# Batches 4 to 7: eight heads' scores in one run on 64 rows of the array, both groups' reads in another, attention recorded visits ahead

## The chip, the cores and the metric

The kernel runs on one core of a Trainium2 chip. The metric is the device time of one execution in microseconds. Three runs of the kernel before gave a median of 700.7 us (698.89 to 702.76).

## The reference, cut to what matters

There are two stages. An attention between 512 tokens and 32 states per head gives, per batch, 544 rows; a gated layer without an activation function runs over all 8 x 544 = 4352 of them.

```
B, H, S, Ns, D = 8, 8, 512, 32, 64            # x: [B, H, S, D], state: [B, H, Ns, D]
scores  = scale * x @ state.T                  # softmax over the states
xread   = softmax(scores) @ state
scores2 = scale * state @ x.T                  # the same scores, turned; softmax over the tokens
sread   = softmax(scores2) @ x
attn = concat([xread, sread], axis=2)          # [B, H, S + Ns, D]
x = attn.transpose(0, 2, 1, 3).reshape(B * (S + Ns), H * D)
out = ((x @ w_a) * (x @ w_b)) @ w_out          # 512 -> 1536 -> 512
```

## The kernel before, in words

**The tokens.** xread is never made. Since xread @ w_a is softmax(scores) @ (state @ w_a), the kernel makes the products P = state @ [w_a, w_b] per head (`project`), writes them to a scratch tensor `scr` in DRAM, and for each batch and chunk c of the 1536 columns reads them back (`p_raw`). `layer1` multiplies them with the weights of the softmax, which stand transposed in `at_h` and `at_l` ([4 heads x 32 states, group, 512 tokens]). Numbers are kept as a high and a low fp32r part, so each product is three matmuls: high x high, high x low, low x high. `layer2` multiplies the gated result (`g_h`, `g_l`) with `w_out` (tiles `wo`), sums over the chunks in four accumulators `acc`, and parks partial sums (`stg`, `part`) between visits.

**The states.** sread is made outright. The reads of all batches gather in the tile `xst`, and `States` runs the gated layer over these 256 rows.

**Attention, per batch and group of four heads** (`Attention`). A batch has two groups, g = 0 and 1. `load` brings x transposed with the states beside it (`x_raw`, 128 rows = two heads x 64). `scores` makes the four heads' scores with four fp32 matmuls into 32 partitions each of one PSUM tile `ms`: all 128 rows of the array are used, and the states of the head that isn't meant are zeros. `soft` takes the maximum over the tokens, and ScalarE the exponential with its sum (tile `e2`, one buffer). In parallel `turn`, `exp`, `norm` and `back` make the token side's softmax and write `at_h` and `at_l`. `reads` transposes the exponentials with four matmuls and copies them to `a2`; `nat` loads x untransposed; `sread` makes the reads with 16 small matmuls (4 token blocks x 4 heads); `scaled` divides by the sum and writes the result twice beside itself; `keep` transposes it with one matmul (`ms<-ident,a`), and two copies of VectorE put it into `xst`.

**The order.** `VISITS` lists which batch does which chunks, and where the states' visits (SU) stand. Batch 4 is first visited in visit 9, batch 5 in 15, batch 6 in 17, batch 7 in 19; the first states' visit is 16. `attend(b)` records a batch's attention just ahead of its first visit, and that of batches 6 and 7 ahead of visit 16, since `tokens` needs all reads. From batch 3 on (`JOINED`) `end_reads(a.scores)` records the reads of the group before and the scores of the next group as one unit, so that TensorE changes only once between its two kinds of matmul.

All work is recorded first, as units with a cost and a due time, and `plan` then orders it: backwards it gives each unit its latest start (`late`), and forwards it picks on each engine the ready unit with the earliest one. The table `SHIFTS` adds a number to the `late` of some runs of units, in hundreds of nanoseconds. `paced` gives the layers' matmuls due times from a clock. Buffers of a name go round in the order of recording; tiles of `stg` (four buffers) and `ms` (two) are free of that order. DMAs are all issued by SP.

Of the kernel before, what the change touches and what calls it, by code (L numbers as in the profile page):

```python
# [20 lines left out]
P = 128  # L21
TOK = S + NS
NG = 2
# [22 lines left out]
WIDE = (0, 1)  # L46

JOINED = 3

# [108 lines left out]
class Unit:  # L158


    def __init__(self, eng):
        self.eng, self.calls, self.acc, self.touch = eng, [], [], []
        self.occ = self.lat = 0.0
        self.base = None
        self.turned = False


class Recorder:
# [31 lines left out]
    def cost(self, u, eng, method, out, ins, kw):  # L200
        n = 1
        sh = (out if isinstance(out, View) else ins[0]).where()[0]
        for x in sh[1:]:
            n *= x
        ps = bool(ins) and ins[0].tile.pool.name.startswith("ps")
        if eng == "PE":
            if method == "transpose" or kw.get("is_transpose"):
                o = n * .85
            elif ins[-1].dtype == F32R:
                o = (n + 32) / 2.4  # L210
            else:
                o = n / .6
            if sh[0] < P:
                o *= sh[0] / P
            if method == "matmul" and "is_transpose" not in kw and ins[-1].dtype == F32 and not u.turned:
                o, u.turned = o + 370, True
            lat = o + 172
        elif eng == "ACT":
            if method == "activation":
                o, lat = (870, 960) if "accum_out" in kw else (560, 660)  # L220
            elif ps:
                o, lat = 466 * n / 512 + (60 if n < 300 else 0), 587 * n / 512 + (80 if n < 300 else 0)
            else:
                o, lat = 522 * n / 512, 100 + n * 1.015
            if n < 8:
                o, lat = 60, 80
        elif eng == "DVE":
            if method.startswith("tensor_scalar") and not ps:
                o, lat = (65, 140) if n <= 1 else (75, 166) if n <= 16 else (333 * n / 512, 419 * n / 512)
            elif method == "tensor_reduce":  # L230
                o, lat = 593, 676
            elif method == "transpose":
                o, lat = 628, 704
            elif method == "reciprocal":
                o, lat = (72, 154) if n == 1 else (162, 244)
            else:
                o, lat = 65 + n * 1.045, 155 + n * 1.045
        elif eng == "SP":
            o = 440
            v = out if isinstance(out, View) else ins[0]  # L240
            u.bytes = 4
            for x in v.where()[0]:
                u.bytes *= x
            u.load = isinstance(out, View) and out.tile.pool.name != "dram"
            u.serve, u.land = u.bytes / 428 + (0 if u.load or u.bytes < 4e5 else 240), 1560 if u.load else 900
            lat = 980 + u.serve + u.land
        else:
            o, lat = 1000, 1060
        if eng in ("ACT", "DVE") and out.tile.name.startswith("sd_") and len(out.where()[0]) == 4:
            o, lat = 2 * o, 2 * lat  # L250
        if eng in ("ACT", "DVE"):
            o, lat = o * SLACK, lat * SLACK
        if u.calls[:-1]:
            u.lat = u.occ + lat
            u.occ += o
        else:
            u.occ, u.lat = o, lat
# [8 lines left out]
class Engine:  # L266
# [13 lines left out]


SHIFTS = {
# [12 lines left out]
}  # L295


# [9 lines left out]
def plan(units, pools, t0):  # L307
# [23 lines left out]
    for p in pools:  # L331
        for tag, tiles in p.tags.items():
            tiles = [t for t in tiles if t.uses]
            for j, t in enumerate(tiles):
                first = min(t.uses)
                opens.setdefault(first, []).append(t)
                for k in set(t.uses):
                    edge(first, k, False)
                if t.free:
                    continue  # L340
                if j:
                    edge(min(tiles[j - 1].uses), first, False)
                if j >= t.bufs and tag not in LOOSE:
                    for k in set(tiles[j - t.bufs].uses):
                        edge(k, first)

    left = [len(x) for x in suc]
    order = [i for i in range(n) if not left[i]]
# [113 lines left out]
def attn_moe(ctx, tc, xt, xn, sd, wl, w_out, out):  # L462
# [26 lines left out]
    def f32(ap):  # L489
        return ap.bitcast(F32)  # L490
# [89 lines left out]

    scr = [[dram.tile([NG, 4, 4, NS, 512], F32, name=f"scr{c}_{g}") for g in range(2)] for c in range(NC)]
    w = {}

# [25 lines left out]
    def project(c, hp, bg, hh, psp, tag):  # L611
        if hh == 0:
            name, bufs = SW[st["n"] % len(SW)]
            st[bg], st["n"] = proj.tile([P, 2, 512], F32, name=name, bufs=bufs), st["n"] + 1
        sw = st[bg]
        ps = psp.tile([P, 512], F32, name=tag)
        with rec.together(sw):
            for cols, r in columns(c, hp, hh):
                for k, s in enumerate((sd_h, sd_l)):
                    nc.tensor.matmul(ps[:, cols], lhsT=s[hp // 2][:, 2 * (hp % 2) + hh, bg], rhs=r,  # L620
                                     start=(k == 0), stop=(k == 1))
        nc.scalar.copy(out=sw[:, hh], in_=ps)
        if hh:
            h = 2 * (hp % 2)
            nxt.extend(lambda i=i: nc.sync.dma_start(
                out=scr[c][bg][hp // 2, :, h + i].rearrange("b n x -> n b x"), in_=sw[:, i]) for i in range(2))


    xst = const.tile([P, 4, B, NS], F32, name="xst")
# [10 lines left out]
    def load_a(b):  # L640
        new_a(b)
        for i in range(2):
            nc.sync.dma_start(out=f32(a_t[b][i]), in_=a_dram[b][i])

    class Attention:

# [15 lines left out]
        def scores(self):  # L662
# [5 lines left out]
            with rec.together(self.e2, *(() if self.b in WIDE else (self.sp,))):  # L668
                for hq in range(4):
                    n = slice(hq * NS, (hq + 1) * NS)  # L670
                    nc.tensor.matmul(self.s[n], lhsT=self.st[:, hq // 2, hq % 2 * NS:(hq % 2 + 1) * NS],
                                     rhs=self.x[:, hq // 2], start=True, stop=True)

        def scores_t(self, psp, tag):

# [62 lines left out]

        def reads(self):
            ps = ps_ms.tile([P, 512], F32, name="ms")  # L740
            self.a2 = att.tile([P, 4, P], F32, name="a2", bufs=1)
            with rec.together(self.a2):
                for sb in range(4):
                    nc.tensor.transpose(ps[:, sb * P:(sb + 1) * P], self.e2[:, sb * P:(sb + 1) * P], ident)
# [20 lines left out]
        def scaled(self):  # L765
            ps, m2 = self.s, self.m2
            nc.vector.tensor_scalar_add(out=m2[:, 3:4], in0=m2[:, 2:3], scalar1=EPS)
            nc.vector.reciprocal(out=m2[:, 3:4], in_=m2[:, 3:4])

            nc.scalar.mul(out=self.a2[:, 0, :].rearrange("p (t d) -> p t d", t=2),  # L770
                          in_=ps[:, :D].unsqueeze(1).broadcast_to([P, 2, D]), mul=m2[:, 3:4])

        def keep(self):
            ps = self.s
            nc.tensor.transpose(ps[:, P:2 * P], self.a2[:, 0, :], ident)
            for hh in range(2):
                rows = slice(hh * D, (hh + 1) * D)
                nc.vector.tensor_copy(
# [137 lines left out]

    clock = [0.0]

    def paced(f, *args):
        u = f(*args[:1], **args[1])  # L920
        u.base = clock[0]
        clock[0] += u.occ * PACE

# [70 lines left out]
    def end_reads(*more):  # L994
# [7 lines left out]
            a.keep()  # L1002
        pending.clear()

    def attend(b):
        if b not in a_t:
            new_a(b)
        for g in range(NG):
            a = atts[b, g]
            a.load()  # L1010
# [73 lines left out]
    for v, (u, cs) in enumerate(VISITS):  # L1084
# [11 lines left out]
        elif not earlier:  # L1096
# [3 lines left out]
                    ready.add(b)  # L1100
            end_reads()
            unit.tokens()
        clock[0] = max(clock[0], STARTS.get(v, 0.0))
        for i, c in enumerate(cs):
            if u != SU:
# [66 lines left out]
```

## Time and profile before

| | before |
|---|---|
| median of three runs | 700.7 us |
| the profiled execution: time | 700.03 us |
| its span, first to last instruction | 698.2 us |
| mean granted clock of TensorE | 0.999 |
| bytes read from and written to HBM | 87.03 and 46.66 MB |

The profile is one execution; its times count from the start of the span. PE is TensorE's matmuls, PEld its weight loads, DVE is VectorE, ACT is ScalarE, SPq SP's queue of DMA issues. A row of the timeline has the start, the time to the end of the last of its instructions, the engine, the line, the operation, the output and input tiles, the shapes and the count. All instructions are issued on one line, 1129, so rows are told apart by tiles. An fp32 matmul leaves two records in the trace, so that 16 matmuls read as x32. A row of the windows has the stretch, then for each engine the busy time and the number of instructions, then the granted clock, the DMA engines' share and GB/s.

### The profile page before, as it was taken

Reading aid. Unit: us, or ns where it says so; the run is one execution under the profiler, and the core shown is the slowest. Engines: PE = TensorE matmul, PEld = TensorE weight load, DVE = VectorE, ACT = ScalarE, POOL = GpSimd, SP = SyncE. Lnnn points to the kernel's source line nnn. Section 1 sums busy time; section 2 is a strip of 40 time slices with the busy share of each in tenths; the row PEclk is TensorE's granted clock in tenths of the full one; section 3 lists DMA queues with packets and bytes.
Section 4 is the critical chain, followed back from the end, with each engine's and each line's share of the span. In section 5 each row is a group of like instructions: output and inputs, shape, how many; then the busy total and the mean of one; then the engine's idle time right before and its main releaser. Section 6 shows DMA issues by size and latency. Waiting matters only on the chain.

```text
span 698.2 us, 10183 instructions
## 1 busy us (share of the span) xinstructions
PE 677.7 (97%) x3712; PEld 543.2 (78%) x3712; DVE 486.5 (70%) x947; ACT 394.3 (56%) x727; POOL 0.7 (0%) x6
## 2 busy tenths in 40 slices
PE   4899999999999999999999999999999999999997
PEld 1576767887878888788888877877798888988886
DVE  5999788889986775745997367558869734884321
ACT  6988967898764667754543344334555433552322
POOL 0000000000000000000000000000000000000000
PEclk9999999999999999999999999999999999999999
DMA  8689977899495757768995144234244312500002
GB/s 325 243 295 336 338 248 243 307 319 393 163 335 204 271 171 251 252 232 263 392 332 158 59 155 125 95 120 139 82 152 150 109 43 61 181 31 30 1 0 92
DMA packets 55090, 134.36 MB, mean 192 GB/s; under 512 B 5632, under 2 KB 5632, under 8 KB 55040
## 3 DMA queue, kind: packets, MB, share of 16 engines
q1 hardware_dynamic: 55040, 133.71, 55.1%
q8 instruction: 29, 0.48, 0.3%
q14 instruction: 21, 0.17, 0.1%
HBM read 87.03 MB, written 46.66 MB: 191 GB/s over the span
## 4 chain that ended last, share of the span: by engine, by line
PE 88%; ACT 5%; DMA 5%; issue 1%; SPq 1%; DVE 0%; DVEq 0%
PE ab L1129 41%; PE acc L1129 38%; PE ms L1129 9%; ACT wq L1129 2%; DMA p_raw<-scr 1%; DMA p_raw<-sd 1%; DMA scr<-sw_st 1%; DMA part<-stg 1%; DMA scr<-wo 1%; SPq L1129 1%; ACT t L1129 1%; ACT sd_h L1129 0%; ACT wo L1129 0%; ACT sw_st L1129 0%; ACT g_h L1129 0%
## 5 line engine op out<-in xcount | busy, mean ns | idle before, releaser
L1129 PE MATMUL acc<-wo,g_h 128*128 128x512 f32 x816 | 249.0, 392 | 0.0
L1129 PEld LDWEIGHTS acc<-wo,g_h 128*128 128x128 f32 x816 | 151.6, 188 | 31.7 <-issue 0.8
L1129 DVE TENSOR_TENSOR a_sb<-ab,a_sb 128x512 f32<-128x512 f32 (+1 forms) x108 | 71.2, 659 | 130.2 <-PE ab L1129 115.2
L1129 PE MATMUL ab<-at_h,p_h 128*128 128x512 f32 x384 | 149.7, 394 | 2.4 <-ACT p_h L1129 2.4
L1129 PE MATMUL acc<-wo,g_l 128*128 128x512 f32 x408 | 150.9, 392 | 0.0
L1129 PE MATMUL ab<-at_l,p_h 128*128 128x512 f32 x384 | 149.6, 393 | 0.0
L1129 PE MATMUL ab<-at_h,p_l 128*128 128x512 f32 x384 | 148.8, 392 | 0.0
L1129 ACT COPY a_sb<-ab 128x512 f32<-128x512 f32 (+1 forms) x108 | 61.0, 565 | 137.6 <-PE ab L1129 137.0
L1129 ACT CAST g_h<-a_sb 128x512 fp32r<-128x512 f32 (+1 forms) x108 | 64.7, 599 | 59.5 <-DVE a_sb L1129 50.1
L1129 PEld LDWEIGHTS acc<-wo,g_l 128*128 128x128 f32 x408 | 76.6, 188 | 19.1 <-issue 2.5
L1129 DVE TENSOR_TENSOR g_l<-a_sb,g_h 128x512 fp32r<-128x512 f32 (+1 forms) x108 | 70.7, 655 | 28.1 <-ACT g_h L1129 21.3
L1129 PEld LDWEIGHTS ab<-at_h,p_h 128*128 128x128 f32 x384 | 72.2, 189 | 23.2 <-ACT p_h L1129 3.5
L1129 PEld LDWEIGHTS ab<-at_h,p_l 128*128 128x128 f32 x384 | 72.3, 189 | 16.0 <-issue 0.8
L1129 PEld LDWEIGHTS ab<-at_l,p_h 128*128 128x128 f32 x384 | 72.2, 189 | 15.3 <-issue 0.8
L1129 ACT CAST p_h<-p_raw 128x512 fp32r<-128x512 f32 x92 | 53.4, 621 | 24.5 <-PE ab L1129 16.0
L1129 DVE TENSOR_TENSOR p_l<-p_raw,p_h 128x512 fp32r<-128x512 f32 x92 | 60.1, 682 | 6.0 <-ACT p_h L1129 5.8
L1129 DVE TENSOR_SCALAR t<-t 128x512 int32<-128x512 int32 x120 | 49.6, 420 | 13.4 <-ACT t L1129 10.8
L1129 ACT CAST wq<-t 64x512 fp32r<-64x512 f32 (+1 forms) x64 | 38.7, 619 | 4.4 <-PE ab L1129 1.7
L1129 DVE SCALAR_TENSOR_TENSOR t<-raw,t 128x512 int32<-128x512 int32 (+1 forms) x60 | 39.5, 684 | 0.2
L1129 PE MATMUL ms<-wq,sd_h 128*128 128x512 f32 (+2 forms) x112 | 38.0, 412 | 0.3 <-ACT a L1129 0.2
L1129 PE MATMUL ms<-wq,sd_l 128*128 128x512 f32 (+2 forms) x112 | 37.4, 403 | 0.0
L1129 DVE TENSOR_TENSOR stg<-acc,stg 128x512 f32<-128x512 f32 x44 | 28.4, 683 | 9.2 <-PE acc L1129 9.2
(97 smaller groups left out, 671.4 us busy)
## 6 DMA issues: line engine op xcount, KB each, us to landing
p_raw<-scr SPq DMA_DIRECT2D x46, 512.0 KB, 4.0
scr<-sw_st SPq DMA_DIRECT2D x48, 256.0 KB, 5.1
scr<-wo SPq DMA_DIRECT2D x48, 256.0 KB, 4.2
raw<-wl SPq DMA_DIRECT2D x22, 512.0 KB, 6.1
part<-stg SPq DMA_DIRECT2D x20, 512.0 KB, 5.6
stg<-part SPq DMA_DIRECT2D x20, 512.0 KB, 5.0
out<-stg SPq DMA_DIRECT2D x34, 256.0 KB, 2.1
x_raw<-xt SPq DMA_DIRECT2D x14, 576.0 KB, 4.0
```

Source lines behind the costliest of these rows:

```text
L1129: getattr(obj, method)(*map(real, args), **{k: real(x) for k, x in kw.items()})
```

## The change

For batches 4 to 7 (`WHOLE = B // 2`) a class `Inputs` and a function `attend_whole` take the place of the steps above.

- **Groups are made anew**: a group is now heads 0, 2, 4, 6 or 1, 3, 5, 7 of the batch, that is, the upper or the lower 64 rows of the loads. The stores to `scr` follow.
- **Scores**: both halves of x are loaded (`x_raw`, and a tile of `stg` with the states in a buffer of `e2`). Eight matmuls of 64 rows follow in one unit: those of rows 0 to 63 into one tile `ms`, those of 64 to 127 into another.
- **Reads**: both groups' x is loaded (`x_nat` and a tile of `stg`), the second group's transposed exponentials go to the buffer of `x_raw`, and all 32 read matmuls are one unit into one tile, 64 columns per group.
- **Scaling and keeping**: each group scales 64 columns, once; one transpose and one copy put both groups into `xst`.
- **When**: `AHEAD` records batch 4 at visit 7, batch 5 at 14 and batch 6 at 15; batch 7 stays ahead of 16. A field `after` keeps a batch's scores behind the last layer matmul that was due by then, and all its units are due 6 us later. The cost of a matmul on 64 rows is halved.
- `SHIFTS` has new numbers for all the program.

```diff
+WHOLE = B // 2
+AHEAD = {7: 4, 14: 5, 15: 6}
...
+            if method == "matmul" and isinstance(kw.get("lhsT"), View) and kw["lhsT"].where()[0][0] < P:
+                o /= 2
...
 SHIFTS = {
-    2: -1852, 7: 155, 8: 101, 12: 125, 13: -1927, 18: -166, 24: 194, 25: 125, 27: 16, 28: -291, 35: 29, 36: 59,
...
+    1: -900, 2: -777, 7: 466, 8: -739, 11: 204, 13: -900, 23: -898, 27: 900, 32: -163, 34: -785, 36: -864, 37:
...
+    for i, u in enumerate(units):
+        if u.after is not None:
+            edge(place[id(u.after)], i, False)
...
-                out=scr[c][bg][hp // 2, :, h + i].rearrange("b n x -> n b x"), in_=sw[:, i]) for i in range(2))
+                out=(scr[c][bg][i, :, hp] if bg else scr[c][bg][hp // 2, :, h + i]).rearrange("b n x -> n b x"),
+                in_=sw[:, i]) for i in range(2))
...
+    class Inputs:
...
+        def load(self):
+            x = att.tile([P, 2, S + D], F32, name="x_raw", bufs=1)
+            nc.sync.dma_start(out=x, in_=xt[self.b, 0])
+            x1 = mlp.tile([P, 2, DM], F32, name="stg", bufs=4)
+            st = att.tile([P, S], F32, name="e2", bufs=1)[:, :2 * D].rearrange("p (a d) -> p a d", a=2)
+            by_halves(nc.sync.dma_start(out=x1, in_=xt[self.b, 1, :, :, :S]))
+            nc.sync.dma_start(out=st, in_=xt[self.b, 1, :, :, S:])
+            self.x, self.st = (x[:, :, :S], x1), (x[:, :, S:], st)
+        def scores(self):
+            self.s = [ps_ms.tile([P, 512], F32, name="ms") for _ in range(2)]
+            with rec.together():
+                for hp in range(4):
+                    for i in range(2):
+                        rows, a = slice(i * D, (i + 1) * D), hp % 2
+                        nc.tensor.matmul(self.s[i][hp * NS:(hp + 1) * NS],
+                                         lhsT=self.st[hp // 2][rows, a, i * NS:(i + 1) * NS],
+                                         rhs=self.x[hp // 2][rows, a], start=True, stop=True)
...
+        def sread(self):
+            self.r = ps_ms.tile([P, 512], F32, name="ms")
+            with rec.together():
+                for g in range(NG):
+                    for sb in range(4):
+                        for hp in range(4):
+                            h = 2 * (hp % 2) + g
+                            nc.tensor.matmul(self.r[hp * NS:(hp + 1) * NS, g * D:(g + 1) * D],
+                                             lhsT=atts[self.b, g].a2[:, sb, hp * NS:(hp + 1) * NS],
+                                             rhs=self.xn[hp // 2][:, sb, h * D:(h + 1) * D],
+                                             start=(sb == 0), stop=(sb == 3))
...
+    def attend_whole(b):
+        inp = Inputs(b)
+        inp.load()
+        inp.scores()
+        begin = clock[0]
+        rec.units[-1].after = [u for u in done_steps if u.base <= begin][-1]
...
+        if v in AHEAD:
+            attend(AHEAD[v])
+            ready.add(AHEAD[v])
```

Where it moves instructions is shown at three places. The first is TensorE at batch 5. Before, a joined run: the reads of one group (`x_nat`, `a`: 16 matmuls) and, right behind, the scores of the next (`x_raw`: 4), with the layers' matmuls (`ab`, `acc`) around them.

```order
L1129 MATMUL ab<-at_l,p_h 128x512
L1129 MATMUL ab<-at_h,p_l 128x512
L1129 MATMUL ms<-x_nat,a_4378 32x64 x16
L1129 MATMUL ms<-x_raw 32x512 x4
L1129 MATMUL ab<-at_h,p_h 128x512
L1129 MATMUL ab<-at_l,p_h 128x512
```

Now the eight scores of batch 5 stand alone.

```order
L1243 MATMUL acc<-wo_2231,g_h 128x512 x2
L1243 MATMUL acc<-wo_2231,g_l 128x512
L1243 MATMUL ms<-x_raw 32x512 x4
L1243 MATMUL ms<-stg,e_2581 32x512 x4
L1243 MATMUL acc<-wo_2231,g_h 128x512 x2
L1243 MATMUL acc<-wo_2231,g_l 128x512
```

The four of `x_raw` are heads 0 to 3, the four of `stg` heads 4 to 7; the 32 reads of the batch follow 55 rows later as a run of their own, and the joined runs of batches 4 to 7 are gone.

The second place is TensorE at the end of batch 7's attention, ahead of the first states' visit: the one transpose of the reads (`ident`, `a`), and what stands behind it up to the first matmul of the states, `ab<-x_nat,wq`, which is the row after the last one shown.

```order
L1243 MATMUL ms<-ident,a_5123 128x128
L1243 MATMUL acc<-wo_3471,g_l 128x512
L1243 MATMUL acc<-wo_3471,g_h 128x512 x2
L1243 MATMUL acc<-wo_3471,g_l 128x512
L1243 MATMUL acc<-wo_3571,g_h 128x512 x2
L1243 MATMUL acc<-wo_3571,g_l 128x512
L1243 MATMUL acc<-wo_3571,g_h 128x512 x2
L1243 MATMUL acc<-wo_3571,g_l 128x512
L1243 MATMUL acc<-wo_3571,g_h 128x512 x2
L1243 MATMUL acc<-wo_3571,g_l 128x512
L1243 MATMUL acc<-wo_3571,g_h 128x512 x2
L1243 MATMUL acc<-wo_3571,g_l 128x512
```

Sixteen matmuls of the second layer stand there; before, that place held 20.

The third is SP's queue at the start of the program. Before, the order was: x of batch 0's first group, two quarters of the weights of chunk 0 (`raw<-wl`), x and states of its second group (`stg<-xt`, twice), the states' two halves (`sd`), two more quarters of the weights.

```order
L1129 DMA x_raw<-xt 128x1152
L1129 DMA raw<-wl 128x1024 x2
L1129 DMA stg<-xt 128x2x512
L1129 DMA stg<-xt 128x2x64
L1129 DMA p_raw<-sd 128x1024 x2
L1129 DMA wo_110<-wl 128x1024
L1129 DMA wo_112<-wl 128x1024
L1129 DMA x_nat<-xn 128x1024
```

Now it is:

```order
L1243 DMA x_raw<-xt 128x1152
L1243 DMA stg<-xt 128x2x512
L1243 DMA stg<-xt 128x2x64
L1243 DMA raw<-wl 128x1024 x2
L1243 DMA wo_106<-wl 128x1024
L1243 DMA x_nat<-xn 128x1024
L1243 DMA p_raw<-sd 128x1024
L1243 DMA wo_112<-wl 128x1024
```

The second group's x and states moved ahead of the weights, the untransposed x ahead of the states' products, and the second half of `sd` to behind five further loads, five rows below the last one shown.

More of the change, by code (lines that the diff above doesn't have):

```diff
@@ L163, in __init__ @@
         self.occ = self.lat = 0.0
-        self.base = None
+        self.base = self.after = None
         self.turned = False
@@ L345, in plan @@
                         edge(k, first)
+    place = {id(u): i for i, u in enumerate(units)}
+    for i, u in enumerate(units):
+        if u.after is not None:
+            edge(place[id(u.after)], i, False)
     left = [len(x) for x in suc]
@@ L643, in load_a, with __init__, nat @@
             nc.sync.dma_start(out=f32(a_t[b][i]), in_=a_dram[b][i])
+    class Inputs:
+        def __init__(self, b):
+            self.b = b
+        def load(self):
[15 more added lines that the diff above has]
+                                         rhs=self.x[hp // 2][rows, a], start=True, stop=True)
+        def nat(self):
+            t = mlp.tile([P, 2, DM], F32, name="stg", bufs=4)
+            self.xn = [att.tile([P, 4, 256], F32, name="x_nat", bufs=1),
+                       t.rearrange("p a x -> p (a x)").rearrange("p (a x) -> p a x", a=4)]
+            for g in range(NG):
+                nc.sync.dma_start(out=self.xn[g], in_=xn[self.b, g])
+        def sread(self):
+            self.r = ps_ms.tile([P, 512], F32, name="ms")
+            with rec.together():
+                for g in range(NG):
+                    for sb in range(4):
[5 more added lines that the diff above has]
+                                             start=(sb == 0), stop=(sb == 3))
     class Attention:
@@ L672, in scores, with begin @@
                                      rhs=self.x[:, hq // 2], start=True, stop=True)
+        def begin(self, inp):
+            self.s = inp.s[self.g]
+            self.e2 = att.tile([P, S], F32, name="e2", bufs=1)
+            self.sp = att.tile([P, 16, 32], F32, name="s_p")
         def scores_t(self, psp, tag):
@@ L740, in reads @@
             ps = ps_ms.tile([P, 512], F32, name="ms")
-            self.a2 = att.tile([P, 4, P], F32, name="a2", bufs=1)
+            if self.b >= WHOLE and self.g:
+                t = att.tile([P, 2, S + D], F32, name="x_raw", bufs=1).rearrange("p a x -> p (a x)")
+                self.a2 = t[:, :S].rearrange("p (a b) -> p a b", a=4)
+            else:
+                self.a2 = att.tile([P, 4, P], F32, name="a2", bufs=1)
             with rec.together(self.a2):
@@ L768, in scaled @@
             nc.vector.reciprocal(out=m2[:, 3:4], in_=m2[:, 3:4])
+            if self.b >= WHOLE:
+                nc.scalar.mul(out=atts[self.b, 0].a2[:, 0, self.g * D:(self.g + 1) * D],
+                              in_=ps[:, self.g * D:(self.g + 1) * D], mul=m2[:, 3:4])
+                return
             nc.scalar.mul(out=self.a2[:, 0, :].rearrange("p (t d) -> p t d", t=2),
@@ L775, in keep @@
             nc.tensor.transpose(ps[:, P:2 * P], self.a2[:, 0, :], ident)
+            if self.b >= WHOLE:
+                nc.vector.tensor_copy(out=xst[:, :, self.b, :], in_=ps[:, P:2 * P].rearrange("p (a n) -> p a n", a=4))
+                return
             for hh in range(2):
@@ L917, in attn_moe @@
     clock = [0.0]
+    done_steps = []
     def paced(f, *args):
         u = f(*args[:1], **args[1])
+        done_steps.append(u)
         u.base = clock[0]
@@ L1003, in end_reads @@
         pending.clear()
+    def attend_whole(b):
[4 more added lines that the diff above has]
+        rec.units[-1].after = [u for u in done_steps if u.base <= begin][-1]
+        first = len(rec.units)
+        for g in range(NG):
+            a = atts[b, g]
+            a.begin(inp)
+            a.soft()
+            a.exp()
+            a.norm()
+            a.back()
+            a.reads()
+        for u in rec.units[first:]:
+            u.base = begin + 6e3
+        inp.nat()
+        inp.sread()
+        for g in range(NG):
+            a = atts[b, g]
+            a.s = inp.r
+            a.scaled()
+        atts[b, 0].keep()
     def attend(b):
@@ L1007, in attend @@
             new_a(b)
+        if b >= WHOLE:
+            end_reads()
+            attend_whole(b)
+            return
         for g in range(NG):
```

27 rows, old and new, of the table SHIFTS are left out of this document.

## The prediction

> **What bounds the kernel now.** I read the head of the page first, then TensorE's own waits, then the timeline of TensorE where the touched work lies.
>
> ```profile
> span 698.2 us, 10183 instructions
> PE 677.7 (97%) x3712; PEld 543.2 (78%) x3712; DVE 486.5 (70%) x947; ACT 394.3 (56%) x727; POOL 0.7 (0%) x6
> PE   4899999999999999999999999999999999999997
> DVE  5999788889986775745997367558869734884321
> ACT  6988967898764667754543344334555433552322
> PE 88%; ACT 5%; DMA 5%; issue 1%; SPq 1%; DVE 0%; DVEq 0%
> ...
> PE ms L1129 <- ACT e L1129: 5.8, 3, 2.3
> PE ms L1129 <- DMA x_raw<-xt: 4.2, 1, 4.2
> PE ab L1129 <- ACT p_h L1129: 2.4, 3, 1.1
> PE acc L1129 <- ACT wq L1129: 2.0, 2, 1.1
> ```
>
> TensorE (PE) is busy for 97% of the span and makes 88% of the chain that ended last. The last four rows are the longest of TensorE's waits (microseconds in all, times, longest); they fit the first digit of its slices, a 4 where the rest are 8 and 9. So there are two kernels in one: a start of some 60 us in which ScalarE and VectorE (the digits 8 and 9 in their first slices) hand TensorE its work too late, and a long rest in which TensorE has no gap that shows. In the rest, time is worth what TensorE's instructions cost, one for one. The three windows below say the same: from 110 on the PE column equals the stretch.
>
> ```profile
> 20.00:45.00 25.00, 22.96 (x200) 15.39 (x199) 23.93 (x57) 23.09 (x49) 0.00 (x0) 1.00 0.70 250
> 110.00:200.00 90.00, 90.00 (x467) 72.68 (x468) 78.42 (x155) 74.67 (x140) 0.00 (x0) 1.00 0.83 289
> 400.00:510.00 110.00, 110.00 (x728) 85.26 (x727) 76.70 (x153) 48.03 (x91) 0.00 (x0) 1.00 0.36 119
> ```
>
> A busy TensorE can't be read from durations, since matmuls overlap; I read starts instead.
>
> ```profile
> 404.68 0.39 PE L1129 MATMUL ab<-at_h,p_h 128*128 128x512 f32 x1
> ...
> 407.18 0.39 PE L1129 MATMUL ab<-at_h,p_l 128*128 128x512 f32 x1
> ...
> 411.06 0.39 PE L1129 MATMUL ab<-at_h,p_l 128*128 128x512 f32 x1
> 411.38 0.65 PE L1129 MATMUL ms<-x_nat,a 128*32 128x64 f32 x32
> 411.85 1.04 PE L1129 MATMUL ms<-x_raw 128*32 128x512 f32 x8
> 412.82 0.50 PE L1129 MATMUL ab<-at_h,p_h 128*128 128x512 f32 x1
> 413.16 0.39 PE L1129 MATMUL ab<-at_l,p_h 128*128 128x512 f32 x1
> ```
>
> Twelve dense matmuls start from 404.68 to 407.18, eleven steps in 2.50 us: 0.227 us each. The rows at 411 are one **joined run** of before: the state reads of one group (16 matmuls, two records each), then the scores of the next group (4 matmuls). From 411.06 to 413.16 are 2.10 us, of which two dense steps are 0.45: the joined run costs 1.65 us. The reads stand from 411.38 to 411.85, 0.47 us; what is left, 1.18 us, is the scores with the change into and out of this kind of matmul.
>
> **The scores, batch by batch.** Of batches 4 to 7, before has eight joined runs, and one run of reads alone behind batch 7; after, that run stands behind batch 3 instead, and cancels. So eight joined runs go: 8 x 1.65 = 13.2 us. In their place come, for each of four batches, one run of eight heads' scores and one run of 32 reads. A run of reads alone is in the trace:
>
> ```profile
> 501.46 0.40 PE L1129 MATMUL ab<-at_l,p_h 128*128 128x512 f32 x1
> 501.79 0.65 PE L1129 MATMUL ms<-x_nat,a 128*32 128x64 f32 x32
> 502.37 0.50 PE L1129 MATMUL ab<-at_h,p_l 128*128 128x512 f32 x1
> 502.71 0.39 PE L1129 MATMUL ab<-at_h,p_h 128*128 128x512 f32 x1
> ```
>
> It costs 502.71 - 501.46 - 0.45 = 0.80 us for one group; a second group behind it in the same run adds its 0.47 without a second change: 1.27 us.
>
> The run of eight heads uses 64 of the array's rows for each head, and no row of the trace has that: every matmul of before uses 128. **Lower bound**: each head still streams its 512 columns, so the run can't be under the 1.18 us of four heads; this is the case that the two row halves work side by side, each into its own accumulator. **Upper bound**: the halves go one after the other, which adds the streaming of another four heads, 1.04 us busy less its 0.18 us of tail (a dense matmul's 0.39 less 0.227 is about that), 0.86 us: 2.04 us. I take the lower one. The nearest row speaks for it: at 411.85 eight records of 512 columns start within 0.97 us, 0.12 us each, where a dense matmul of 512 columns takes 0.227; so parts of the array that differ in their columns do work at once already. Then a batch costs 1.18 + 1.27 = 2.45 us, four cost 9.8, and the difference is 9.8 - 13.2 = **-3.4 us**. With the upper bound it is 0.0.
>
> The Trainium skill, in "TensorE: Matmul & The Clock Gate", section "Measured speedup vs the span model", gives 3.07 for four row tiles and not 4; as an estimate by that page, two halves would need 1/0.77 of the ideal streaming of 0.86 us, 0.26 us more a run, and the sum would be -2.4. The same page and "TensorEngine Tiling (Array Packing)", "Gotcha 1: PSUM Pressure", allow row tiles at once only into different banks; the code gives each half its own tile, and no run here has shown it yet.
>
> **The transposes that keep the reads.** One per batch goes away, since both groups' reads stand in one tile.
>
> ```profile
> 460.80 0.28 PE L1129 MATMUL ms<-ident,a 128*128 128x128 f32 x1
> 460.83 0.71 PE L1129 MATMUL acc<-wo,g_h 128*128 128x512 f32 x2
> 461.39 0.39 PE L1129 MATMUL acc<-wo,g_l 128*128 128x512 f32 x1
> ```
>
> From 460.80 to 461.39 are 0.59 us, two dense steps are 0.45: 0.14 us each, four times, **-0.55 us**. The transposes of the exponentials (four matmuls per group) stay as many.
>
> **What moves on the other engines.** ScalarE runs as many instructions as before; VectorE loses twelve copies of some 0.22 us (the row at 504.98 below has two in 0.45). Neither counts, as TensorE is the bound there. SP issues four loads more. They are hidden: the DMA engines are at 0.36 in the window 400:510 where three of the four batches lie. If that cover were gone, a pair of such loads holds SP's queue for 1.2 to 1.9 us (rows 2.12 and 10.01 below).
>
> The change adds waits on TensorE: its queue stands still behind a run of scores until all of a batch has landed, and behind a run of reads until both groups' exponentials are turned. The tightest place is batch 7, since the states' visit needs it next. Before, that end looks so:
>
> ```profile
> 494.25 0.69 DVE L1129 TENSOR_REDUCE m<-ms 128x1 f32<-128x512 f32 x1
> ...
> 496.53 0.69 ACT L1129 ACTIVATE e<-ms,m 128x512 f32<-128x512 f32 x1
> ...
> 504.10 0.27 PE L1129 MATMUL ms<-ident,a 128*128 128x128 f32 x1
> ...
> 504.98 0.45 DVE L1129 COPY xst<-ms 64x64 f32<-64x64 f32 x2
> ...
> 506.15 1.05 ACT L1129 CAST x_nat<-xst 128x1024 fp32r<-128x1024 f32 x1
> ...
> 508.77 0.40 PE L1129 MATMUL ab<-x_nat,wq 128*128 128x256 f32 x2
> ```
>
> From the last transpose, at 504.10, the work needs some 0.3 us, a copy of 0.2 and a cast of 1.05, about 2 us with its hand-overs. In the new order 16 dense matmuls stand there, 3.6 us. Ahead of it, the score run and the first group's transposes are 19 dense matmuls apart, 4.3 us, for a maximum of 0.69 and an exponential of 0.69 us (the first two rows), with a small bias between them and the hand-overs: covered, also where the second group's maximum stands in between. I cost these waits at nothing.
>
> **The start.** The new table also reorders the first 60 us, which hold nothing of batches 4 to 7. The trace prices what stands first there:
>
> ```profile
> 4.25 1.93 PE L1129 MATMUL ms<-x_raw 128*32 128x512 f32 x8 [4.25 <-DMA x_raw<-xt]
> ...
> 1.19 0.89 SPq L1129 DMA_DIRECT2D raw<-wl  x2
> 2.12 1.87 SPq L1129 DMA_DIRECT2D stg<-xt  x2
> ...
> 10.01 1.20 SPq L1129 DMA_DIRECT2D stg<-xt  x2
> ...
> 7.22 0.66 ACT L1129 ACTIVATE t<-raw 128x512 f32<-128x512 f32 x1 [4.88 <-DMA raw<-wl]
> 7.78 0.57 ACT L1129 COPY e<-ms 128x512 f32<-128x512 f32 x1
> ...
> DMA to landing us min/median/max: 3.5/4.0/9.2
> ```
>
> After, the two activation loads (1.87 us of SP's queue) go ahead of the two weight loads, so the first weights land 1.9 us later, at 9.1; but the copy of the first scores no longer stands behind them, and can start at about 6.3, where TensorE's scores end (4.25 + 1.93), and not at 7.78. Loss and gain are of one size. Bounds: +1.9 if all of ScalarE waits for the weights, -1.5 if the earlier copy carries through, and another -2.4 if the 2.4 us that TensorE waits for p_h later go too. I take 0, as the two rows that point to each side are about equal.
>
> **Sum.** -3.4 - 0.55 + 0 = -4.0 us. The profiled execution took 700.03 us (span 698.2 and 1.8 around it): 700.03 - 4.0 = **696.0**. The median of the runs shown is 700.7, 0.7 above it, so the same step from the median would give 696.7; I stay with the profiled one.
>
> **Rivals.**
> - *The row halves go one after the other*, or the halves' writes get in each other's way. For it: no row shows 64 rows in use. Against it: columns already work side by side. The runs then cost 2.04 + 1.27 us, the sum is -0.6: **699.5**.
> - *The start gains*: the order of the first 60 us lets the attention of batch 0 begin earlier, and the later waits for p_h vanish. Of the -3.9 that was bounded above half or all goes with it: **692 to 694**. For it speaks that all the idle time of TensorE is there; against it that ScalarE and VectorE are full in that stretch (23.09 and 23.93 of 25 us), and no work of theirs there is removed.
> - *The start loses, and the kernel gets slower*: the weights, now behind the activations, land late. The longest landing of such an activation load was 9.2 us where the median is 4.0. If the weights behind it are 5.2 + 1.9 = 7.1 us later, ScalarE has batch 0's copies and exponentials to fill with, 2 to 3 us (a copy of 0.57 and an exponential of 0.69 for each of two groups), and some 4 to 5 us are left over; from 4.0 on it eats the gain. With the serial halves it would decide from 0.6 on. Time: **700 to 704**.
> - *The change does what it says but a batch's chain turns into a wait*, at one or two of the four batches, by the missing 1 us each: 697 to 698; I count it in the forecast's own range.
>
> **How the numbers follow.** About 0.5%, 3.5 us, is what a measurement of this kernel can tell from no change. The forecast, 694 to 698, gets 0.52; it lies astride the limit of 696.5, so 0.31 of it is faster and 0.21 the same. The serial halves get 0.18, all the same. The gain at the start gets 0.18, all faster. The loss at the start gets 0.12: 0.09 slower, 0.03 the same. So faster 0.49, same 0.42, slower 0.09. The range leaves out the far half of the gain at the start and of the loss: 691.5 to 700.5.
>
> **What would show each step.** In the trace of after, a run of eight scores should stand between two dense matmuls with about 1.2 us taken (2.0 by the first rival), with 16 records whose first eight start within some 50 ns. A run of 64 read records should take about 1.3 us. The transposes with the identity of the reads should be 12, not 16. TensorE's waits should still be the 5.8, 4.2, 2.4 and 2.0 us and little else. I would be wrong most likely by the start: if TensorE's rows turn dense over 2 us earlier or later than now, that moves the end by as much.

## The result, and the profile after

| | before | after |
|---|---|---|
| median | 701.73 us (698.89 to 703.89, 4 runs) | 708.87 us (707.51 to 710.07, 4 runs) |
| span of the profiled execution | 698.2 us | 707.3 us |

The ratio is 1.0104, with a 95% interval of 1.006 to 1.0147: the changed kernel is slower, by some 7 us, where 4 less were predicted.

The first rows answer to those of before: the head of the page of after, the summary of its chain, and TensorE's longest waits (us in all, times, longest).

```profile
span 707.3 us, 10143 instructions
PE 678.4 (96%) x3708; PEld 543.7 (77%) x3708; DVE 481.5 (68%) x935; ACT 393.8 (56%) x727; POOL 0.7 (0%) x6
PE   4798899999999999999999999999999999999997
PE 85%; DMA 7%; ACT 6%; DVE 1%; issue 1%; SPq 0%; ACTq 0%
...
PE ab L1243 <- ACT p_h L1243: 4.5, 3, 2.6
PE ms L1243 <- DMA x_raw<-xt: 4.4, 1, 4.4
PE ms L1243 <- ACT e L1243: 3.8, 4, 2.2
PE ab L1243 <- ACT a_sb L1243: 2.4, 2, 1.8
PE acc L1243 <- ACT wq L1243: 2.4, 1, 2.4
PE ms L1243 <- ACT sw_st L1243: 1.7, 2, 1.3
```

TensorE's share of the chain fell from 88% to 85%, and DMA's grew from 5% to 7%. The span is 9.1 us longer, while TensorE was busy for only 0.7 us more: the other 8.4 are waits, in which it stood idle. Three of the rows (`a_sb`, `sw_st`, the larger `p_h`) were not there before.

Where they are, the windows tell: the first two rows are of before, the next four of after. Columns: the stretch, its length, busy time (and instructions) of PE, PEld, DVE, ACT and POOL, the granted clock, the DMA engines' share, GB/s.

```profile
0.00:60.00 60.00, 45.13 (x359) 28.72 (x359) 49.70 (x114) 46.35 (x89) 0.70 (x6) 1.00 0.82 298
60.00:110.00 50.00, 48.79 (x339) 34.25 (x338) 41.84 (x87) 40.61 (x76) 0.00 (x0) 1.00 0.81 285
...
0.00:60.00 60.00, 42.31 (x311) 27.29 (x312) 47.22 (x107) 44.84 (x87) 0.70 (x6) 0.88 0.78 277
60.00:110.00 50.00, 47.48 (x298) 34.45 (x300) 38.71 (x78) 37.05 (x68) 0.00 (x0) 0.97 0.76 266
110.00:200.00 90.00, 86.10 (x469) 67.12 (x462) 67.88 (x133) 66.85 (x125) 0.00 (x0) 1.00 0.77 269
400.00:510.00 110.00, 110.00 (x646) 87.81 (x645) 65.41 (x128) 42.97 (x82) 0.00 (x0) 1.00 0.34 113
```

Before, TensorE was busy for all of the 90 us from 110 to 200; now it lacks 3.9 there, 2.5 of the 50 us ahead of it (1.2 before), and 17.7 of the first 60 (14.9 before). From 400 on, where three of the four changed batches lie, it has no gap in either kernel.

Next is the touched work itself, in TensorE's timeline of after: the eight scores of a batch, then the end of a run of 64 read records.

```profile
428.27 0.39 PE L1243 MATMUL acc<-wo,g_l 128*128 128x512 f32 x1
428.59 0.63 PE L1243 MATMUL ms<-x_raw 64*32 64x512 f32 x4
428.61 0.63 PE L1243 MATMUL ms<-stg,e 64*32 64x512 f32 x4
429.04 0.61 PE L1243 MATMUL ms<-x_raw 64*32 64x512 f32 x4
429.07 0.61 PE L1243 MATMUL ms<-stg,e 64*32 64x512 f32 x4
429.61 0.72 PE L1243 MATMUL acc<-wo,g_h 128*128 128x512 f32 x2
430.17 0.40 PE L1243 MATMUL acc<-wo,g_l 128*128 128x512 f32 x1
...
299.72 0.39 PE L1243 MATMUL ab<-at_h,p_l 128*128 128x512 f32 x1
300.03 0.25 PE L1243 MATMUL ms<-x_nat,a 128*32 128x64 f32 x2
...
300.91 0.23 PE L1243 MATMUL ms<-stg,x_raw 128*32 128x64 f32 x2
301.06 0.50 PE L1243 MATMUL ab<-at_h,p_h 128*128 128x512 f32 x1
301.40 0.40 PE L1243 MATMUL ab<-at_l,p_h 128*128 128x512 f32 x1
```

From 428.27 to 430.17 are 1.90 us, of which three dense steps are 0.68: the scores cost **1.22 us**, predicted 1.18. The reads cost 301.40 - 299.72 - 0.45 = **1.23 us**, predicted 1.27. So the touched work does what was forecast. The loss is elsewhere.

To follow it, I work out TensorE's **lost time** from its records: the start of an instruction, less the time that all matmuls ahead of it need at the steps of undisturbed stretches (0.227 us for 512 columns, in proportion for others, and the runs of small matmuls as just measured). It holds waits and half-speed stretches alike; only its growth and its differences mean something. It is an estimate: with the median step between each two kinds of matmul in place of these lengths, the differences below come out 0.5 to 1.4 us smaller, in the same places. Counted so, the work itself is 649.3 us before and 645.7 after: 3.6 us less.

| lost time, us, at | 60 | 110 | 160 | 200 | 240 | 400 | 690 |
|---|---|---|---|---|---|---|---|
| before | 29.8 | 36.8 | 36.8 | 38.4 | 38.3 | 39.4 | 44.8 |
| after | 33.7 | 42.0 | 48.1 | 49.7 | 52.7 | 53.5 | 57.5 |
| difference | 3.9 | 5.2 | 11.3 | 11.3 | 14.4 | 14.1 | 12.8 |

The 12.8 us lost less the 3.6 us saved is what the span grew by (9.1). TensorE's busy time should have fallen by the 3.6 too, and it rose by 0.7. I put this down to stretches at half the granted clock, in which the same work counts as busy for longer (0.88 is the mean of the first 60 us); they are named below. Of the 12.8, 11.3 are there by 160 us. The first changed instruction on TensorE, batch 4's scores, runs at 228.6 us. So most of the loss lies in work that is the same in both kernels.

Rows of after with new waits (in brackets: idle time before the instruction, and who ended it):

```profile
58.40 0.50 PE L1243 MATMUL ab<-at_h,p_h 128*128 128x512 f32 x1 [2.62 <-ACT p_h L1243]
...
84.56 0.50 PE L1243 MATMUL ab<-at_h,p_h 128*128 128x512 f32 x1 [1.79 <-ACT a_sb L1243]
...
115.09 0.50 PE L1243 MATMUL ab<-at_h,p_h 128*128 128x512 f32 x1 [1.71 <-ACT p_h L1243]
...
146.48 0.50 PE L1243 MATMUL ms<-wq,sd_h 128*128 128x512 f32 x1 [1.30 <-ACT sw_st L1243]
```

The one at 115.09 can be followed back. These are the pieces of after's chain there (start, length), and the loads of `p_raw` around it in the view of that tile, of after from 100 to 115.6 us and then of before from 95 to 118 us (after has three loads from 95 to 118, the first of them at 110.7).

```profile
103.79 6.73 DMA scr<-wo
110.72 3.69 DMA p_raw<-scr
```

```profile
L1243 SPq DMA_DIRECT2D p_raw<-scr x2: 372/418/463, 110.7 to 111.1; - x2
```

```profile
L1129 SPq DMA_DIRECT2D p_raw<-scr x4: 368/377/463, 102.3 to 112.3; - x4
```

In after the products go to the scratch tensor at 103.8 and are asked back at 110.7, as soon as they are there; TensorE waits for the round trip through DRAM. In before such loads went out from 102.3 on, and TensorE had no gap at that place. I read this as a question of order: the products are made late. The counts agree: from 110 to 150 us ScalarE makes 10 copies of products (`sw_st`) in before and 4 in after.

Two theories, then. **A**: the new order of untouched work costs the 12.8 us, and with a good order the new shape is worth its 3.6 to 4. **B**: the new shape needs this (larger loads, both `ms` tiles taken at once, an attention visits ahead), and its table only makes the best of it.

### The profile page after: what moved, and what is told of

It is laid out like the page before. It is cut to its first block, busy times and chain, and to the rows that moved or that the text cites. A ratio compares the mean times of both kernels' runs of the same rounds, so it can differ in the third digit from the quotient of the medians.

```text
span 707.3 us, 10143 instructions
## 1 busy us (share of the span) xinstructions
PE 678.4 (96%) x3708; PEld 543.7 (77%) x3708; DVE 481.5 (68%) x935; ACT 393.8 (56%) x727; POOL 0.7 (0%) x6
## 4 chain that ended last, share of the span: by engine, by line
PE 85%; DMA 7%; ACT 6%; DVE 1%; issue 1%; SPq 0%; ACTq 0%
PE ab L1243 40%; PE acc L1243 36%; PE ms L1243 8%; DMA scr<-wo 3%; DMA p_raw<-scr 2%; ACT wq L1243 1%; DMA p_raw<-sd 1%; DMA wo<-wl 1%; ACT t L1243 1%; ACT e L1243 1%; ACT wo L1243 1%; ACT p_h L1243 1%; SPq L1243 0%; DVE stg L1243 0%; ACT sw_st L1243 0%
## 5 line engine op out<-in xcount | busy, mean ns | idle before, releaser
L1243 PE MATMUL acc<-wo,g_h 128*128 128x512 f32 x816 | 254.3, 392 | 0.6 <-ACT g_h L1243 0.6
L1243 PE MATMUL ab<-at_h,p_h 128*128 128x512 f32 x384 | 151.9, 398 | 7.0 <-ACT p_h L1243 4.5
L1243 PE MATMUL acc<-wo,g_l 128*128 128x512 f32 x408 | 154.2, 392 | 0.0
L1243 PEld LDWEIGHTS ab<-at_h,p_l 128*128 128x128 f32 x384 | 72.7, 189 | 14.9
L1243 PE MATMUL ms<-wq,sd_h 128*128 128x512 f32 (+2 forms) x112 | 38.6, 417 | 2.4 <-ACT sw_st L1243 1.7
L1243 DVE SCALAR_TENSOR_TENSOR t<-raw,t 128x512 int32<-128x512 int32 (+1 forms) x60 | 39.7, 684 | 0.1
L1243 ACT COPY sw_st<-ms 128x512 f32<-128x512 f32 x44 | 25.8, 592 | 15.0 <-PE ms L1243 13.3
```

The source lines that it names most:

```text
L1243: getattr(obj, method)(*map(real, args), **{k: real(x) for k, x in kw.items()})
```

## The experiments

Each ratio is against the kernel before on the same chip, with its 95% interval.

**E1 and E8: the old numbers in the new kernel.** In E1 all numbers for the part of the recording that both programs share (runs below 633) are before's, in E8 only the first (below 260).

```diff
 SHIFTS = {
-    1: -900, 2: -777, 7: 466, 8: -739, 11: 204, 13: -900, 23: -898, 27: 900, 32: -163, 34: -785, 36: -864, 37:
+    2: -1852, 7: 155, 8: 101, 12: 125, 13: -1927, 18: -166, 24: 194, 25: 125, 27: 16, 28: -291, 35: 29, 36: 59,
```

> The kernel after, with the numbers of the kernel before in the table for runs of units below 633 (the first unit that the two programs do not share is in run 633), and its own numbers from there on. Theory A, the loss of 12.8 us that piles up before the first scores on 64 rows at 228 us is made by the table's new numbers for work that the change does not touch: the loss goes, and the 4 us of TensorE's work stay won, 694 to 699. Theory B, the new shape of batches 4 to 7 (recorded visits ahead, its loads, its due times) holds the early work up whatever the numbers: 706 to 710.

> The kernel after, with the numbers of before in runs below 260 only, which hold the first 60 us. If the loss of the start (3.9 us of slack at 60 us, half of it by TensorE's clock at half speed till 32 us) is the work of those numbers alone: slack at 60 us back to about 30 us. The total tells whether it also stays won: 703 to 706 if the later order is not hurt by it, 707 to 712 if the rest of the table fits only its own start.

E1 took 707.43 us (ratio 1.0082, 1.0052 to 1.0111), E8 708.49 (1.0114, 1.0084 to 1.0144). Neither got the time back, though both repaired what they were aimed at: at 60 us the lost time was 30.6 and 29.8, as before. E1 was still at 39.7 at 160, but then it lost 9.4 us up to 240, of which these TensorE rows are a part:

```profile
173.35 0.50 PE L1238 MATMUL ms<-wq,sd_h 128*128 128x512 f32 x1 [1.85 <-ACT sw_st L1238]
...
214.06 0.68 PE L1238 MATMUL ab<-at_h,p_h 128*128 128x512 f32 x1 [0.50 <-ACT p_h L1238]
...
229.08 0.66 PE L1238 MATMUL ms<-ident,e 128*128 128x128 f32 x4 [0.75 <-ACT sw_st L1238]
```

E1's time lies in the range of theory B, E8's in the one given for a rest of the table that fits only its own start. Yet they don't decide for B, since numbers are not an order. They shift due times in a plan that also knows of batch 4's early attention, and the same numbers then give another order: in E1 TensorE's matmuls stand as in before up to 63 us, and from there on they don't.

**E2: the new numbers in the old kernel**, the reverse of E1.

> The kernel before, with the numbers of the kernel after in the table for runs of units below 633, its own from there on. Theory A: it loses what after loses before 228 us, and wins nothing: 709 to 714. Theory B: it stays at 699 to 703.

It took 715.18 us (1.0174, 1.0128 to 1.0219). The old shape, with no changed attention anywhere, loses 34.7 us by 60 and 51.8 by 160, as after does and somewhat more; the time is a little over A's range. TensorE's matmuls stand in the order of after up to 81 us. So the new numbers are enough to make the loss without the new shape, which speaks for A.

**E3 and E4: no table**, in the new and in the old kernel.

```diff
 SHIFTS = {
-    1: -900, 2: -777, 7: 466, 8: -739, 11: 204, 13: -900, 23: -898, 27: 900, 32: -163, 34: -785, 36: -864, 37:
...
+}
```

> The kernel after with an empty table. To be read against the next one, the kernel before with an empty table, which gives the price of the new shape with no numbers on either side. Theory A: about 4 us faster than the next one. Theory B: about 8 us slower than the next one. Both may be some per cent slower than with a table.

> The kernel before with an empty table: 705 to 735 by either theory, which differ in how it stands to the kernel after with an empty table (theory A: 4 us slower than that; theory B: 8 us faster).

They took 725.26 us (1.034, 1.029 to 1.0389) and 724.67 (1.0328, 1.0296 to 1.036): alike, and inconclusive. The lost time at 690 is 74.7 and 70.3 us; without a table both kernels are some 24 us slower than before, and a difference of 4 us between the shapes can hide in what two such poor orders happen to lose.

**E5 to E7: searched tables, miswritten.** A table searched for the new kernel (E5), one for the old (E6), and one for the new from another start (E7). Their numbers were written a hundred times too large.

> The kernel after, its table searched anew (from its own numbers, by the planner's own costs), nothing else changed. Theory A, the new shape of batches 4 to 7 saves its 4 us of TensorE's work and the loss is in the order that the table makes of all the other work: well under before, 690 to 697, with TensorE's slack before 228 us back near the 38 us of before. Theory B, the new shape itself makes waits that no numbers take away: 702 to 709.

> The kernel before, its table searched in the same way and from the same numbers of after, as a control: what a search alone gives. Theory A: 694 to 700, 3 to 5 us above the kernel after with a searched table, which is the price of the old scores. Theory B: at or below the kernel after with a searched table.

> The kernel after with a second searched table, started from the mixture of the first experiment (early numbers of before). Theory A: again under before, 691 to 698, so that the result hangs on no single table. Theory B: 702 to 709.

They took 766.17, 734.64 and 769.77 us (1.0932, 1.0498 and 1.098). These are far above every range that was given. They say only what a poor order costs, 5 to 10%, and nothing of the shapes.

**E9: the old order itself in the new kernel.** Due times in place of numbers: each instruction that before plans in its first 175 us gets its place there, so that every engine's order up to there is before's. All later ones keep the places that after plans for them.

```diff
+RANKS = [
...
         late[i] = d + shift[i]
+        if i < len(RANKS) and RANKS[i] is not None:
+            d = RANKS[i] * 10.0
```

(The added lines stand ahead of the one that sets `late`, and `SHIFTS` is empty.)

> The changed kernel, but on every engine the first 175 us stand in the order that the kernel before has them in (each instruction's due time is its place in that order); behind it the changed kernel's own order. All of this work is the same in both kernels; batch 4's scores come later. Theory A (the lost time is the order's of untouched work, the new shape saves TensorE 3.6 to 4 us): the time that TensorE has lost by 170 us is before's, some 37 us and not the 48 of the changed kernel, the waits for p_h at 58, 84 and 115 and for sw_st at 146 go, and the total is 708.9 - 11 = 698 us (695 to 701). Theory B (what the new shape needs, larger loads, both score tiles, an attention visits ahead, is what holds up TensorE): the loss is found again by 240 us in other places, total 705 to 709.

It took **696.16 us** (694.65 to 698.4; before 700.91; ratio 0.9935, 0.9913 to 0.9956): at the medians 4.8 us faster than before and 12.7 faster than after, with the new shape complete. TensorE's matmuls do stand as in before, up to 159 us. The profiled execution is the slowest of the five (698.40 us; its span, 696.4, is 1.8 under before's), so the rows below are those of a slower one. TensorE's waits and three windows of it:

```profile
PE ms L1527 <- ACT e L1527: 5.7, 3, 2.6
PE ms L1527 <- DMA x_raw<-xt: 4.4, 1, 4.4
PE ab L1527 <- ACT p_h L1527: 2.9, 2, 2.0
PE acc L1527 <- ACT wq L1527: 1.8, 2, 1.2
PE ms L1527 <- DVE s_p L1527: 1.7, 1, 1.7
PE ms L1527 <- ACT a L1527: 0.2, 1, 0.2
```

```profile
60.00:110.00 50.00, 48.79 (x306) 34.91 (x304) 40.73 (x85) 39.77 (x74) 0.00 (x0) 0.99 0.84 287
110.00:200.00 90.00, 90.00 (x462) 73.35 (x461) 74.82 (x144) 70.51 (x129) 0.00 (x0) 1.00 0.83 290
200.00:260.00 60.00, 59.88 (x275) 47.35 (x274) 49.10 (x95) 40.79 (x74) 0.00 (x0) 1.00 0.70 244
```

The waits are nearly those of before; `a_sb` and `sw_st` are gone. From 110 to 200 TensorE is full again, and from 200 to 260, where batch 4's early scores stand, it lacks 0.12 us. The lost time is 38.6 at 160, 40.8 at 240 and 45.7 at 690 (before: 36.8, 38.3, 44.8). So theory B falls: in this order the shape doesn't hold TensorE up by more than about 1 us, neither by its loads nor by its two tiles.

**E10 and E11: the searched tables in the right unit**, for the new and the old kernel, with an equal search.

> The changed kernel with a table searched for it (E5 to E7 had each number of their search a hundred times too large, so they say nothing of the shapes; here the numbers are in the unit of the search). Theory A: with an order of its own that is good, the shape shows its 3.6 to 4 us: 2 to 5 us faster than the next run, and faster than the changed kernel by 8 us or more (692 to 700). Theory B: no faster than the next run, 702 to 708.

> The kernel before with a table searched for it in the same way and for as long. Theory A: 696 to 703, 2 to 5 us slower than the run before this one. Theory B: 696 to 703, as fast as it or faster.

E10 took 695.28 us (0.9922, 0.9897 to 0.9946), E11 697.72 (0.9956, 0.9931 to 0.998). Each kernel with its own good order is faster than before, and the new shape is the faster by 2.4 us at the medians; the intervals overlap, so the size of this step is not certain. The profiled spans, 693.4 and 698.1, differ by 4.7, but the profiled execution of E11 (700.1 us) is one of its slowest.

**E12: a table for the new kernel that also had to bear delays.**

> The changed kernel with a table searched on: each order was also judged with every duration varied by some 4% and every load landing up to a microsecond or two late. Theory A (the shape is worth 3.6 to 4 us and an order can be found that loses little else): at least as fast as the earlier searched table, 691 to 696 us, TensorE's waits under 16 us in all. Theory B (what was gained in E9 and E10 is the lucky fit of one order): back to 698 or more.

It took 695.10 us (693.95 to 696.47, 6 runs; 0.9922, 0.9908 to 0.9935). That beats both kernels, and lies level with E10 and E9: three different orders come out at 695 to 696, so it isn't the lucky fit of one order. TensorE waits for 18.3 us in its ten longest rows, 7.0 of them for the first load; that is more than the 16 expected.

## Why the prediction was wrong

- **Eight joined runs for four runs of scores and four of reads: right.** The sum per batch was taken as 2.45 us, and measured as 1.22 + 1.23 = 2.45. The row halves work side by side: the first rival (2.04 us a run) didn't come. By the estimate from the Trainium skill, "TensorE: Matmul & The Clock Gate", section "Measured speedup vs the span model", 0.26 us a run would have come on top of the bound; 0.04 did.
- **One transpose less per batch: right in number**, 12 where 16 were. All of TensorE's work fell by 3.6 us as counted above, against 3.95 forecast.
- **The waits that the change adds: right at nothing, or nearly.** With before's order ahead of them (E9) TensorE lacks 0.12 us from 200 to 260 and 0.04 from 400 to 510.
- **"The start ... I take 0": wrong, and the rival "the start loses" too small.** By 60 us 3.9 us are lost, over the +1.9 of the bound. That bound priced two loads ahead of the weights, and both rows behind it came as priced: in after ScalarE starts on the weights at 9.01 (forecast 9.1) and on the copy of the first scores at 6.36 (about 6.3). What came late also was the second half of `sd`, which SP, in before's timeline, issued right behind the first:

```profile
4.03 1.63 SPq L1129 DMA_DIRECT2D p_raw<-sd  x2
```

  In after it stands in the chain at 11.46:

```profile
11.46 8.80 DMA p_raw<-sd
```

  It is there at 20.3 (11.46 + 8.80), in before at about 12.8 (issued at 5.1, 7.7 to land). A matmul that reads a half of `sd`, the row doesn't tell which, starts at 22.17, and at 21.40 in before:

```profile
22.17 1.94 PE L1243 MATMUL acc<-wq,p_raw 128*32 128x256 f32 x16 [2.38 <-ACT wq L1243]
```

  The trace names `wq` as what ended this wait, and no engine as one that waited for `sd`; so that `sd` made it is not shown. Another part is TensorE's clock, which no wait tells of. The granted clock of after is 0.50 from 20 to 30 us, and its dense matmuls start 0.43 us apart up to 31.5; those of before are at 0.23 from 27.5 on. Two rows of before, then two of after:

```profile
27.52 0.62 PE L1129 MATMUL ab<-at_h,p_h 128*128 128x512 f32 x2
27.98 0.39 PE L1129 MATMUL ms<-at_h,wo 128*128 128x512 f32 x1
...
29.38 0.63 PE L1243 MATMUL ab<-at_l,p_h 128*128 128x512 f32 x1
29.80 0.63 PE L1243 MATMUL ab<-at_h,p_l 128*128 128x512 f32 x1
```

  After is busy from 27.6 to 31.9 at that pace, 4.3 us, of which about half is lost: by this estimate up to 2.1 us. The prediction has no term for it.
- **"In the rest, time is worth what TensorE's instructions cost, one for one": this step failed, and with it the prediction.** It is true of an order in which ScalarE, VectorE and the round trips through DRAM are far enough ahead, and that order was changed too: the new table has numbers all over the program. I took it as harmless beyond 60 us because the work there is untouched; that it is the same work says nothing of when its products are made. From 60 to 240 us another 10.5 us of lost time came (14.4 less 3.9), and later 1.6 went again. In the profile of before there was a hint of its price: from 110 to 200 ScalarE and VectorE are busy for 74.67 and 78.42 of 90 us, so TensorE runs without a gap there only while each of their instructions comes in time.
- **The number itself.** With the order held (E9), 696.16 us stand against 696.0 predicted. That it fits to 0.2 us is in part luck: at the medians E9 gains 4.8 us, its profiled execution 1.6 (698.40 against 700.03), and with both kernels tuned the shape is worth 2.4 (E10, E11). The terms of the touched work were right, and the term for the table, which should have been a rival of its own with 10 us or more to lose, was missing.

What remains open: which of the moved instructions makes which wait, beyond the one at 115 us, was not traced. Nor did any run combine the old order with a single part of the change, so the 4.8 us of E9 are split between scores, reads and transposes only by the rows of the trace.

## What to carry to other kernels

A table that tunes an order belongs to the program that it was tuned on: when a change renews it, price the table as an edit of its own, over the whole program and not only near the changed code. To know what a change of shape is worth, hold the order of everything else (the order itself, since the same numbers in a changed plan give another one), or tune both sides alike. And where TensorE is full only because two other engines at 83 to 87% are always in time, "one for one" is an upper end of the gain, not its value.

## What the runs showed of the hardware

**Row halves work side by side.** The 16 records of eight fp32 heads on 64 x 32 parts of the array start as two waves of eight; each of the rows at 428.59 and 428.61 holds matmuls of both row halves, and eight heads cost 1.22 us where four heads on all rows cost 1.18.

**A wait can be paid twice.** After the 2.62 us of waiting that ended at 58.40, the granted clock falls to half for 3.4 us (a mean of 0.57 over 4 us), while TensorE is full; the windows of after around it:

```profile
56.00:59.00 3.00, 0.60 (x3) 0.51 (x4) 1.91 (x5) 1.27 (x3) 0.00 (x0) 1.00 0.98 287
59.00:63.00 4.00, 4.00 (x32) 2.97 (x34) 3.57 (x9) 3.58 (x8) 0.00 (x0) 0.57 1.04 425
```

That costs up to 1.7 us on top (half of 3.4), and no view of waits names it: the page counts TensorE as busy there. In E9 a wait of 1.97 us that ended at 56.55 was followed by the same, a granted clock of 0.50 from 58 to 61. The length of one wait doesn't decide it: in E8 a wait of 2.03 us ended at 116.01, and the granted clock stayed at 1.00 from 113 to 123; in E1 it was 0.50 from 214.2 to 217.6, behind two waits of 0.51 and 0.50 us.
